# Tiny products of zeros at the start of a scan and expert-layer kernel, and a later line for a load

## The chip, the cores and the metric

The kernel runs on one core of a Trainium2 chip. A core has five engines that run at the same time, each working through its own list of instructions in order: TensorE (PE) multiplies matrices, VectorE (DVE), ScalarE (ACT) and GpSimd (POOL) work element by element, and SyncE (SP) mostly issues transfers (DMAs) between the main memory and the core's own. Engines wait for each other through semaphores. A product on PE is a weight load (shown as PEld) and a matmul that streams columns through the loaded weights; in fp32 each product is made in two such passes.

The metric is the device time of one execution in microseconds. The kernel before takes 350.53 us, the median of three runs (350.33 to 351.12).

## The reference

Inputs are x (4 batches, 8 heads, 768 steps, 32 wide), a (one decay per step), B and C (16 wide), and two weights, w_in (256 x 2048) and w_out (2048 x 256). All is fp32.

```python
for c in range(S // 32):                      # the scan, per batch and head
    cum = np.cumsum(log_a[c])
    L = np.exp(cum[:, None] - cum[None, :]) * causal
    y_intra = ((C_c @ B_c.T) * L) @ x_c
    y_inter = (C_c @ state) * np.exp(cum)
    y[c] = y_intra + y_inter
    state = exp(sum(la)) * state + sum_j(B_j x_j * exp(cum[-1] - cum_j))
h = y_as_rows @ w_in                          # 3072 rows of 256
g = np.where(h > 0, h, np.exp(np.minimum(h, 0)) - 1)
out = g @ w_out
```

So a scan along the sequence makes 3072 rows of 256 numbers, and a two-layer network with an elu in between is applied to every row.

## The kernel before, in words

The 3072 rows are cut into twelve blocks of 256 steps, numbered n = 0 to 11; `place(n)` gives batch and third of the sequence. Within a block the scan works in chunks of 64 steps (Q) for all eight heads. For a block it needs B and C turned so that their 16 columns lie along partitions (`turn`, L422, or `turn_square`, L446), the decays L (`first_decays`, L505, for blocks 0 and 1 and `decay_of`, L518, later), the scores C times B (`scores`, L532), which are weighed by L (`weigh`, L547), the new states (`sums`, L562, and `states`, L578), and then the two halves of y: `across` (L604) with the state from before the chunk and `inside` (L624) with the weighed scores. `scores`, `sums`, `across` and `inside` are bursts of many small products, each on its own part of PE's array: one block's `inside` is 32 products, which are 64 weight loads and 64 matmuls in the trace; for two blocks, and in two steps t, it is 64 and 64 for each t.

The network follows block by block. `l1` (L659) and, from block 2 on in two-block pairs, `l1_words` (L777) make h; the elu is spread over ACT and DVE; `l2` (L820) and `second` (L866) make the output, the latter by a scheme of seven products of quarters.

No scheduler orders the work: inside `tc.manual_schedule()` each engine carries out its instructions in the order in which the source names them. Waits come from the reuse of buffers and from the data.

Three places matter here.

**The start.** L257 to L268 make a tile of zeros (`idle`), whose products PE computes into a bank that nobody reads: `idle_product(4)` and `idle_product(3)`, with 512 and 384 columns. On PE they stand ahead of the first scan: `first_low` (L475, its products are L481), `first_cum` (L486, products L492 and L500), the turned decays of `turned` (L360, product L364) and `turn` (L422, products L428). Beside them DVE computes the running sum of log a (L320), and then takes PE's results: L369 (eb), L436 (the masked C), L550 (`weigh`), and, in the same order, the conversion of the weights (L231, L223, L238). POOL adds the two halves of a converted weight at L248, which `l1` (product L667) waits for. A third `idle_product(3)` stands at L1001.

**The pairs of blocks.** From L1302 on, pair n is put through l1_words and second in sixteen steps k = 0 to 15, and the scan of the next pair m = n + 2 is woven in: at k = 9 `scores`, `sums`, `weigh_two` and the first `states`, at k = 13 `across` and `inside` with eight matmuls of `second` between the bursts.

**The loads.** `stage_scan` (L1282) issues the scan's transfers and ACT's decays for the next pairs. At k = 10 it issues, for both blocks of the pair after the next (m + 2 and m + 3), `load_b` (L135, tile `b`, two buffers) and `spread_cum` (L377, tile `L`, two buffers). They are issued from SP, which carries them out when the buffer's last readers are done: for `b` the products of `sums` (L571), for `L` the products of `weigh` on DVE.

Of the kernel before, what the change touches and what calls it, by code (L numbers as in the profile page):

```python
# [18 lines left out]
Q = 64  # L19
# [13 lines left out]
def kernel(  # L33
# [27 lines left out]
    nc = tc.nc  # L61
# [3 lines left out]
    NP = NB * NG  # L65
# [26 lines left out]
    for k in range(4):  # L92
        (nc.scalar if k % 2 else nc.sync).dma_start(
            out=la0[BH * k:BH * (k + 1)],
# [26 lines left out]
    def load_bc(n, c_queue=nc.sync, us=(0, 1)):  # L121
        b, g = place(n)
        if "bc" not in st.setdefault(n, {}):
            st[n]["bc"] = raw.tile([P, 2, 2, NH, N], F32, tag="bc", name="bc", bufs=2)
        if n > 3:
            for k in range(2):
                load_squares(n, k)
            return
        for u in us:
            sl = slice((2 * g + u) * P, (2 * g + u + 1) * P)  # L130
            for k, src in enumerate((B,) if n == 1 else (B, C)):
                (nc.sync, c_queue)[k].dma_start(
                    out=st[n]["bc"][:, k, u], in_=src[b, :, sl, :].rearrange("h s n -> s h n"))

    def load_b(n):  # L135
        b, g = place(n)
        st.setdefault(n, {})["b"] = raw.tile([P, 2, NH, N], F32, tag="b", name="b_tok", bufs=2)
        for u in range(2):
            sl = slice((2 * g + u) * P, (2 * g + u + 1) * P)
            nc.sync.dma_start(  # L140
                out=st[n]["b"][:, u], in_=B[b, :, sl, :].rearrange("h s n -> s h n"))

    def load_x(n, piece=None):
        b, g = place(n)
        st[n]["x"] = raw.tile([P, 2, NH * D], F32, tag="xr", name="xr", bufs=3)
        for u in range(2):
            sl = slice((2 * g + u) * P, (2 * g + u + 1) * P)
            nc.sync.dma_start(
                out=st[n]["x"][:, u].rearrange("p (h d) -> p h d", d=D),
                in_=x[b, :, sl, :].rearrange("h s d -> s h d"))  # L150
            if piece is not None and u == 0:
                w_load(piece)
# [104 lines left out]
    idle = att.tile([P, P], F32, tag="M", name="idle", bufs=8)  # L257
    nc.vector.memset(idle, 0.0)
    ps_idle = p_o.tile([P, 4, P], F32, tag="o", name="ps_idle")

    def idle_product(k):

        nc.tensor.matmul(
            out=ps_idle[:, 0:k], lhsT=idle, rhs=idle.unsqueeze(1).to_broadcast([P, k, P]),
            start=True, stop=True)

    idle_product(4)
    idle_product(3)  # L268
    ident = const.tile([P, P], F32, name="ident")
    make_identity(nc, ident)  # L270
# [8 lines left out]
    for v in range(2):  # L279
        nc.gpsimd.affine_select(  # L280
            out=low16[Q * v:Q * v + Q], in_=low16[Q * v:Q * v + Q], pattern=[[1, Q]],
# [5 lines left out]
        out=hmask, in_=hmask, pattern=[[-N, NH]], compare_op=ALU.is_ge, fill=0.0,  # L287
        base=0, channel_multiplier=1)
    nc.gpsimd.affine_select(
        out=hmask, in_=hmask, pattern=[[N, NH]], compare_op=ALU.is_ge, fill=0.0,  # L290
# [8 lines left out]
        out=minus, in0=ident, scalar1=-1.0, scalar2=None, op0=ALU.mult)  # L299
# [77 lines left out]
    def spread_cum(n):  # L377

        st.setdefault(n, {})["L"] = L = att.tile([P, NH, 2, Q], F32, tag="L", name="L", bufs=2)
        b, g = place(n)  # L380
        for v in range(2):
            nc.sync.dma_start(
                out=L[Q * v:Q * v + Q].rearrange("p h u i -> p (h u i)"),
                in_=flat[g, v, NH * b:NH * (b + 1)].rearrange("h u i -> (h u i)").unsqueeze(
                    0).to_broadcast([Q, NH * P]))

    def spread_exp(n):

        st.setdefault(n, {})["ec"] = ec = att.tile([P, 2, P], F32, tag="ec", name="ec", bufs=4)
        nc.sync.dma_start(  # L390
            out=ec.rearrange("p u i -> p (u i)"),
            in_=flat_exp[rows_of(n)].unsqueeze(1).to_broadcast([NH, N, BLK]))
# [9 lines left out]
    def scaled(n, eng):  # L402

        s = st[n]
        s["sc"] = sc = s["b"] if n > 3 else raw.tile(
            [P, 2, NH, N], F32, tag="b", name="sc", bufs=2)
        factor = eb0[:, :, NH * n:NH * (n + 1)] if n < 2 else eb[:, :, rows_of(n)]
        eng.tensor_tensor(
            out=sc, in0=s["b"] if n > 3 else s["bc"][:, 0],
            in1=factor.unsqueeze(3).to_broadcast([P, 2, NH, N]), op=ALU.mult)  # L410
# [107 lines left out]
    def decay_of(n, h):  # L518
        L, row = st[n]["L"], rows_of(n).start + NG * h
        for u in range(2):  # L520
            nc.scalar.activation(  # L521
                L[:, h, u], L[:, h, u], ACT.Exp, bias=ncum[:, u, row:row + 1])
        if h % 4 == 3:
            for v in range(2):
                part = L[Q * v:Q * v + Q, h - 3:h + 1]
                nc.gpsimd.affine_select(  # L526
                    out=part, in_=part, pattern=[[0, 4], [0, 2], [1, Q]],
                    compare_op=ALU.is_ge, fill=0.0, base=0, channel_multiplier=-1)
# [753 lines left out]
    def stage_scan(n, k):  # L1282

        m = n + 2
        if k < 2:
            spread_exp(m + k)
        if k == 2:
            load_x(m)
            load_x(m + 1)
        heads = ((5 + 3 * k) // 2, (8 + 3 * k) // 2) if n == 4 else (2 * k - 2, 2 * k)  # L1290
        for h in range(*heads) if 0 < k < 9 else ():
            decay_of(m + h // NH, h % NH)
        if k in (7, 8):
            scaled(m + k - 7, nc.gpsimd)
        if k in (6, 7) and m + 2 < NP:
            load_bc(m + k - 4)
        if k == 10 and m + 2 < NP:
            for to in (m + 2, m + 3):
                load_b(to)
                spread_cum(to)  # L1300

    for n in range(4, NP, 2):  # L1302
        m = n + 2 if n + 2 < NP else None
# [6 lines left out]
        for k in range(16):  # L1310
# [9 lines left out]
            if m:  # L1320
                stage_scan(n, k)
# [64 lines left out]
```

## Time and profile before

| | |
|---|---|
| median of three runs | 350.53 us (350.33 to 351.12) |
| the profiled execution, own time | 350.53 us |
| its span, first to last instruction | 348.6 us |
| PE busy | 341.0 us (98%) |
| DVE, ACT, POOL busy | 257.9, 234.7, 216.5 us |
| instruction queues | q8 30 packets, q14 17 packets |
| PE's products of zeros, first two | 1.10 to 4.45 us |

A line of a timeline gives the start, the length, the engine, the line of the source, the operation, the tiles written and read, the shape, the number of instructions, and in brackets the engine's idle time before it and what ended it. A line of the list of waits gives who waited for whom, the time in all, how often, and the longest. Group lines end with the busy time, the mean duration in ns, and the idle time before. A busy PE is not a PE at its peak: matmuls overlap, and their ends are modelled.

### The profile page before, as it was taken

How to read it: one execution, taken by the hardware profiler on the slowest of the kernel's cores; microseconds unless marked ns; L12 is line 12 of the kernel's file. 1: busy time of each engine (PE TensorE's matmuls, PEld its weight loads, DVE VectorE, ACT ScalarE, POOL GpSimd, SP SyncE). 2: the span in 40 equal slices, each digit the busy share in tenths (PEclk: the TensorE clock that was granted, in tenths of full speed). 3: DMA queues.
4: the chain of work that ended last, by engine and by line, in shares of the span. 5: the costliest groups of instructions: out<-in, count | busy, mean ns of one | idle time of the engine just before them, and what ended most of it. 6: DMA issues, size and time to landing. Idle time of an engine off the chain costs nothing.

```text
span 348.6 us, 9875 instructions
## 1 busy us (share of the span) xinstructions
PE 341.0 (98%) x3878; PEld 298.4 (86%) x3878; DVE 257.9 (74%) x515; ACT 234.7 (67%) x537; POOL 216.5 (62%) x338
## 2 busy tenths in 40 slices
PE   8899999999999999999999999999999999999996
PEld 5579888888778899888999888899988999999996
DVE  3998989889997899876788675878775756665232
ACT  4789989598658988557599457599457466565000
POOL 5554554539998699965296665196754174455760
PEclk9999999999999999999999999999999999999999
DMA  8988989371360510170421070420000100001002
GB/s 146 240 214 173 294 168 261 86 140 42 66 139 0 129 40 17 18 152 2 108 60 32 9 156 7 105 34 2 2 0 5 62 0 3 0 0 51 14 0 62
DMA packets 72727, 26.49 MB, mean 76 GB/s; under 512 B 57768, under 2 KB 67560, under 8 KB 72680
## 3 DMA queue, kind: packets, MB, share of 16 engines
q1 hardware_dynamic: 70360, 25.60, 31.8%
q8 instruction: 30, 0.49, 0.6%
q10 hardware_dynamic: 2320, 0.26, 0.6%
q14 instruction: 17, 0.14, 0.1%
HBM read 22.51 MB, written 3.34 MB: 74 GB/s over the span
## 4 chain that ended last, share of the span: by engine, by line
PE 87%; ACT 3%; DVE 3%; SPq 2%; DMA 2%; issue 1%; POOL 0%; POOLq 0%; ACTq 0%
PE ps_o L902 36%; PE ps_h L787 18%; PE ps_h L667 11%; PE ps_w L787 9%; PE ps_o L827 6%; PE ps_y L634 2%; DMA w<-in_moe_w_in_dram 2%; PE ps_g L541 2%; PE ps_y L616 1%; PE ps_st L571 1%; DVE ps_h L794 1%; ACT e L800 1%; SPq L178 1%; ACT yT L651 1%; ACT e L801 1%
## 5 line engine op out<-in xcount | busy, mean ns | idle before, releaser
L902 PEld LDWEIGHTS ps_o<-w_out,g 128*128 128x128 f32 x640 | 78.5, 191 | 3.5
L902 PE MATMUL ps_o<-w_out,g 128*128 128x128 f32 x640 | 80.1, 275 | 0.0
L800 ACT ACTIVATE e<-ps_h 128x512 f32<-128x512 f32 x72 | 43.0, 597 | 47.2 <-DVE ps_h L794 47.2
L808 DVE SCALAR_TENSOR_TENSOR g<-e,ps_h 128x512 f32<-128x512 f32 x72 | 49.3, 685 | 31.9 <-ACT e L801 30.4
L843 POOL TENSOR_TENSOR g<-g 128x256 f32<-128x256 f32 x36 | 27.3, 758 | 58.5 <-DVE g L808 58.4
L794 DVE SCALAR_TENSOR_TENSOR ps_h<-ps_h,e 128x512 f32<-128x512 f32 x72 | 50.1, 695 | 13.2 <-ACT e L791 10.3
L791 ACT ACTIVATE e<-ps_w 128x512 f32<-128x512 f32 x72 | 42.2, 586 | 20.1 <-PE ps_w L787 20.0
L787 PE MATMUL ps_w<-y_both,w_words 128*128 128x512 f32 x144 | 51.7, 438 | 0.1
L801 ACT ACTIVATE e<-e 128x512 f32<-128x512 f32 x72 | 45.5, 632 | 2.3
L667 PE MATMUL ps_h<-yT,w_in 128*128 128x256 f32 (+1 forms) x208 | 45.1, 367 | 1.6 <-POOL w_in L248 1.6
L787 PE MATMUL ps_h<-y,w_words 128*128 128x512 f32 x144 | 45.7, 399 | 0.0
L787 PE MATMUL ps_h<-y,w 128*128 128x512 f32 x144 | 45.0, 392 | 0.0
L667 PEld LDWEIGHTS ps_h<-yT,w_in 128*128 128x128 f32 x208 | 36.4, 190 | 7.2 <-POOL w_in L248 2.3
L521 ACT ACTIVATE L<-L,ncum 128x64 f32<-128x64 f32 x160 | 42.2, 336 | 0.1
L902 PE MATMUL ps_o<-w_sum,g 128*128 128x128 f32 x304 | 38.6, 276 | 0.0
L902 PEld LDWEIGHTS ps_o<-w_sum,g 128*128 128x128 f32 x304 | 37.0, 192 | 1.4
L526 POOL TENSOR_SCALAR_AFFINE_SELECT L<-L 64x512 f32<-64x512 f32 x40 | 29.3, 733 | 8.0 <-ACT L L521 6.7
L787 PEld LDWEIGHTS ps_h<-y,w 128*128 128x128 f32 x144 | 27.0, 188 | 7.0 <-POOL w L843 0.4
L787 PEld LDWEIGHTS ps_h<-y,w_words 128*128 128x128 f32 x144 | 26.6, 188 | 6.2 <-issue 0.5
L843 POOL TENSOR_TENSOR g<-t,g 128x256 f32<-128x256 f32 x40 | 28.2, 737 | 5.8 <-PE ps_o L902 5.7
L827 PE MATMUL ps_o<-w_out,g 128*128 128x256 f32 x128 | 30.4, 381 | 0.0
L843 POOL TENSOR_TENSOR g<-g,t 128x256 f32<-128x256 f32 x40 | 28.6, 748 | 0.2
(133 smaller groups left out, 536.5 us busy)
## 6 DMA issues: line engine op xcount, KB each, us to landing
L<-flat SPq DMA_DIRECT2D x20, 256.0 KB
w<-in_moe_w_out_dram SPq DMA_DIRECT2D x8, 512.0 KB
w<-in_moe_w_in_dram SPq DMA_DIRECT2D x7, 512.0 KB
xr<-in_x_dram SPq DMA_DIRECT2D x24, 128.0 KB
out_dram<-c_sum SPq DMA_DIRECT2D x9, 256.0 KB
bc<-in_B_dram SPq DMA_DIRECT2D x24, 64.0 KB
bc<-in_C_dram SPq DMA_DIRECT2D x22, 64.0 KB
ec<-flat_exp SPq DMA_DIRECT2D x10, 128.0 KB
```

Source lines behind the costliest of these rows:

```text
L521: nc.scalar.activation(L[:, h, u], L[:, h, u], ACT.Exp, bias=ncum[:, u, row:row + 1])
L526: nc.gpsimd.affine_select(out=part, in_=part, pattern=[[0, 4], [0, 2], [1, Q]], compare_op=ALU.is_ge, fill=0.0, base=0, channel_multiplier=-1)
L667: nc.tensor.matmul(out=ps[:, j, toks], lhsT=w_in[i][:, k, j * P:(j + 1) * P], rhs=yT[n // 2][:, k, n % 2].rearrange("p u i -> p (u i)")[:, ...
L787: nc.tensor.matmul(out=ps, lhsT=lhs[:, k], rhs=rhs[:, k], start=k == 0 and lhs is not w0, stop=k == KC - 1 and lhs is not w1)
L791: nc.scalar.activation(e, both, ACT.Copy, scale=WORD)
L794: nc.vector.scalar_tensor_tensor(out=high, in0=high, scalar=WORD - 1.0, in1=e, op0=ALU.mult, op1=ALU.add)
L800: nc.scalar.activation(e, high, ACT.Relu, scale=-1.0)
L801: nc.scalar.activation(e, e, ACT.Exp, scale=-1.0)
L808: nc.vector.scalar_tensor_tensor(out=g_of[n, m].rearrange("p b i -> p (b i)"), in0=e, scalar=1.0, in1=h, op0=ALU.subtract, op1=ALU.max)
L827: nc.tensor.matmul(out=o_of[n][:, ts], lhsT=g_of[n, j][:, m % 2, ts * P:(ts + 1) * P], rhs=w_out[:, m], start=(m == 0 and ts == 0), stop=( ...
L843: nc.gpsimd.tensor_tensor(out=out, in0=in0, in1=in1, op=ALU.subtract)
L902: nc.tensor.matmul(out=ps[:, ts], lhsT=b[:, ts * P:(ts + 1) * P], rhs=a[:, i], start=(i == chunk[0] and ts == 0), stop=(i == chunk[-1]), s ...
```

## The change

Two edits. The first product of zeros has 384 columns instead of 512, and behind it stand 29 new products of zeros: weights of 32 rows and 64 columns, 16 columns streamed, in turn into the upper and the lower half of the columns of the array. Each is an fp32 product, so it puts four records into PE's list, 116 in all. The other edit moves the loads of `b` and `L` for the pair after the next from step 10 to step 13 in the source.

```diff
+    def small_idle_products(count):
+
+        for k in range(count):
+            cols = slice(Q * (k % 2), Q * (k % 2) + Q)
+            nc.tensor.matmul(
+                out=ps_idle[cols, 0, 0:16], lhsT=idle[0:32, 0:Q], rhs=idle[0:32, 0:16],
+                start=True, stop=True, tile_position=(0, Q * (k % 2)), skip_group_check=True)
+
-    idle_product(4)
+    idle_product(3)
+    small_idle_products(29)
     idle_product(3)
...
-        if k == 10 and m + 2 < NP:
+        if k == 13 and m + 2 < NP:
             for to in (m + 2, m + 3):
                 load_b(to)
                 spread_cum(to)
```

## The prediction

> **What bounds the kernel now.** I read the page first, then the list of waits, then PE's timeline at the waits, then the start of PE and DVE.
>
> ```profile
> PE 341.0 (98%) x3878; PEld 298.4 (86%) x3878; DVE 257.9 (74%) x515; ACT 234.7 (67%) x537; POOL 216.5 (62%) x338
> ...
> q8 instruction: 30, 0.49, 0.6%
> ...
> PE 87%; ACT 3%; DVE 3%; SPq 2%; DMA 2%; issue 1%; POOL 0%; POOLq 0%; ACTq 0%
> ```
>
> PE is the bound: 98% busy, 87% of the chain that ended last. Queue q8 brings instructions: 30 packets of 16,384 bytes (0.49 MB). PE idles in few places, and two lines of the list of waits hold them:
>
> ```profile
> PE ps_y L634 <- issue: 1.6, 4, 0.6
> ...
> PE ps_h L667 <- POOL w_in L248: 1.6, 3, 0.8
> ```
>
> The first is what the change aims at. "issue" means that the engine waited for nothing that the profile shows. PE's timeline at the second of the four (start, length, instruction):
>
> ```profile
> 156.88 0.86 PE L634 MATMUL ps_y<-M,xr 64*32 64x64 f32 x64
> 157.66 0.71 PE L902 MATMUL ps_o<-w_sum,g 128*128 128x128 f32 x4
> 158.31 0.48 PE L634 MATMUL ps_y<-M,xr 64*32 64x64 f32 x33
> 159.14 0.46 PE L634 MATMUL ps_y<-M,xr 64*32 64x64 f32 x31 [0.35 <-issue]
> 159.53 0.73 PE L787 MATMUL ps_w<-y_both,w_words 128*128 128x512 f32 x2
> ```
>
> Two equal bursts of `inside`; the second breaks off after 33 of 64. I counted PE's records (weight loads, products, waits) up to each of the four breaks: 2753, 4033, 5313, 6593, that is 1280 = 5 x 256 apart, and 256 records of 64 bytes are one packet of q8. The packets that start ahead of the breaks do so at 100.56, 156.54, 209.38 and 262.21 us, and the breaks end 2.90, 2.60, 2.34 and 2.72 us later (103.46, 159.14, 211.72, 264.93). So I read: PE's records come in blocks of 256, the next block is fetched when PE enters one, some 3.5 us pass from the crossing until it can be used (about 0.9 to the packet, then these 2.3 to 2.9), and only `across` and `inside` burn 256 records faster.
>
> The start, PE's timeline again:
>
> ```profile
> 1.10 3.35 PE L263 MATMUL ps_idle<-idle 128*128 128x512 f32 x4 [1.10 <-DVE idle L258]
> 4.25 1.06 PE L481 MATMUL ps_x<-low,ident 128*128 128x256 bf16 x4
> 5.24 1.16 PE L492 MATMUL ps_x<-first,ident 32*64 32x128 f32 x32
> 6.33 1.03 PE L500 MATMUL ps_x<-minus,first 32*128 32x128 f32 x16
> 7.19 0.25 PE L364 MATMUL ps_eb<-ident,first 32*128 32x32 f32 x2
> ...
> 15.29 0.60 PE L481 MATMUL ps_x<-low,ident 128*128 128x256 bf16 x4
> 15.82 0.69 PE L492 MATMUL ps_x<-first,ident 32*64 32x128 f32 x32
> 16.44 0.73 PE L500 MATMUL ps_x<-minus,first 32*128 32x128 f32 x16
> ...
> 23.02 1.99 PE L667 MATMUL ps_h<-yT,w_in 128*128 128x256 f32 x8 [0.49 <-POOL w_in L248]
> ```
>
> The same work takes 1.06 us at 4.25 and 0.60 at 15.29: the array runs at half rate first. The products of L263 start 849 and 638 ns apart for 512 and 384 columns, 1.66 ns a column; later 256 columns take 214 ns, 0.84 a column. The trace's clock record has full rate from 7.01 us on.
>
> DVE's timeline shows who waits for this start:
>
> ```profile
> 7.50 0.23 DVE L369 TENSOR_SCALAR eb<-ps_eb 128x64 f32<-128x64 f32 x1 [1.99 <-PE ps_eb L364]
> ...
> 15.77 0.70 DVE L231 TENSOR_SCALAR ps_mag<-ps_mag 128x512 f32<-128x512 f32 x1 [0.16 <-ACT ps_mag L196]
> ```
>
> From 7.50 to the mag of L238 at 20.80 DVE works in order nearly without a hole; that mag releases POOL's L248 at 21.64 and this PE at 23.02, and then PE has no gap over 0.06 us until 103. So what delays L364 delays everything, less DVE's one hole of 0.16.
>
> **The change part by part.**
>
> Load moved from step 13 instead of 10: nothing. In what is built, every engine has the same instructions in the same order, SP included (no other transfer lies between the two steps), and every wait is for the same event; only counts of PE's semaphore are 29 higher. The loads are released by PE's L571 and the readers of L, as before. Bounds 0 and 0.
>
> The shift. 29 fp32 products are 58 weight loads and 58 products, 116 records; the smaller first product keeps its records. In the old numbering the block edges move from 193+256k to 77+256k. Old times of the new edges round the four places: 92.29, 102.03, 108.28; 150.38, 157.30, 165.29; 204.18, 210.03, 217.07; 258.25, 262.97, 270.88. The closest pair anywhere is 4.7 us, above 3.5, so all four breaks should go. Worth: the unbroken burst lasts 157.66 - 156.88 = 0.79 to the next instruction; the broken ones 1.22 (159.53 - 158.31), 1.17 (212.30 - 211.13) and 1.34 (265.32 - 263.99). Gain 0.43 + 0.38 + 0.55 = **1.36 us**, with PE the chain behind each. The first break (0.56) I cost at nothing: ACT and DVE bound that stretch.
>
> ```profile
> 103.13 0.63 ACT e L801
> 103.76 0.26 ACT yT L651
> ```
>
> ACT goes from L801 straight into six copies that end at 105.96; those of the second burst begin at 104.8, when PE had been done since 104.3, and PE waits for y_both at 115.3 anyway. Were that cover gone, 0.65 more is gained.
>
> The Trainium skill (Runtime: NRT & Kernel Launch, Instruction fetch mechanics) also has blocks of 16 KiB, 256 instructions, but gives PE room for 2048 and calls a crossing mostly hidden. By it the breaks are no fetches, the gain is 0, and the sum below is 353.6; the spacing of 1280 records speaks against it.
>
> The tiny products. Old: streaming from 1.27, L481 at 4.25. New, at half rate: two passes of 384 columns, 1.28, to 2.54; the change of shape 0.14 (L481 to L492: 349 ns apart, of which 212 stream), 2.68. Then 58 pairs of a 64-column load and a 16-column product, on two column halves in turn. No row shows a product shorter than its load. The loads by shape:
>
> ```profile
> L902 PEld LDWEIGHTS ps_o<-w_out,g 128*128 128x128 f32 x640 | 78.5, 191 | 3.5
> ...
> L616 PEld LDWEIGHTS ps_y<-bct,Sx 32*64 32x64 f32 x352 | 5.0, 131 | 2.5 <-POOL Sx L593 1.6 <-POOL w_sum L843 0.3
> ```
>
> 64 columns more cost 60 ns at full rate, and in L616's first round the second product of a tile starts 54 ns after its load does. So a load of 64 columns streams for 54 ns, 107 at half rate, and the next product on that half must wait for it; the two halves overlap, as the tiles of L634 do (8 products in 56 ns). 29 rounds of 0.11 = 3.2 us. Bounds: 0.4 (58 at L634's 6.7 ns) and 6.2 (58 x 107, halves not overlapping). I take 3.2, since two tiles, not eight, are in turn and the load is the longer part. The products end at 5.87; with 0.16 out of the shape, 0.21 for a full load and 1.28 for the second product(3), L481 starts at 7.55 if the clock is still at half rate, 3.3 later than 4.25.
>
> The clock decides the rest. Before the switch PE had streamed from 1.27 to 7.01, 5.7 us. The new stretch from 2.7 to 6.3 streams 16 columns per load, a quarter to a half of the time. If that counts as work, the switch stays at 7.0: the second product ends at 7.28, L481, L492 and L500 take 0.53 + 0.62 + 0.66 = 1.81 as at 15.29, L364 is at 9.1, 1.9 late. If it doesn't, they take about 2.9 as before and L364 is at 10.4, 3.25 late; with a full 5.7 us from 6.27 the switch would come at 12.0 and cost up to 0.9 more. I take 3.25: work at a third of the rate is nearer to none. Less DVE's 0.16: **+3.1 us**.
>
> The Trainium skill (TensorE: Matmul & The Clock Gate, Part 1) says that the gate looks at free-running windows of 3413 ns and opens after a busy one. The trace agrees: full rate lasted 341.33 us, 100 windows. By it the window 0.18 to 3.59, with PE streaming for 68%, did not suffice, and a missed one at 7.01 means 10.42.
>
> Sum: the profiled execution took 350.53 (span 348.6, 1.9 round it), which is also the median. 350.53 - 1.36 + 3.1 = **352.3 us**. A measurement tells about 0.2%, 0.7 us, from no change.
>
> **Rivals.**
>
> Clock on time: 350.53 - 1.36 + 1.9 - 0.16 = 350.9. For it: weight loads run all the time. Against: the columns streamed.
>
> Faster: the tiny products pass at burst pace, because loads on a quarter of the rows do not hold up the next product. At 0.4 to 0.85 us (6.7 ns as L634, 14.6 as L616) L481 comes 0.5 to 0.9 late, the clock stays at 7.0, and L364 is about 0.6 late: 350.53 - 1.36 + 0.4 = 349.6. It decides when the 58 pairs take under about 1.0 us. For it: all bursts in the trace run so. Against: those use four or eight tiles and products at least as long as their loads.
>
> Halves take turns: 6.2 us of tiny products. L364 is 5.2 late: 354.2. For it: both halves read the same 32 rows. Against: L634 overlaps four column tiles on the same rows.
>
> The shift doesn't do what it says (the breaks belong to the burst, or others open at the new edges): 352.3 + 1.36 = 353.6. The spacing of 1280 speaks against it.
>
> **How the numbers follow.** Forecast 0.40 (alone 351.6 to 353.2), clock on time 0.20, burst pace 0.22, halves in turn 0.11, no gain 0.07. Forecast, halves and no gain are slower: 0.58. Burst pace is faster but for its upper end: 0.20. The clock rival and that upper end are the same: 0.22. The range leaves out most of the halves in turn and the lower part of burst pace: 349.4 to 353.8.
>
> **What would show it.** Right: no "issue" wait at L634; L481 first at about 7.5 and L364 near 10.4 against 7.19; L481's first four at half rate; DVE's L369 3 us late; the rest shifted as a block, about 1.7 later at the end. Wrong: L481 before 5.5 (burst pace), L492 at 0.69 us length (clock on time), a break in L541, L571 or L634 at another place (edges), or PE's waits at 23 gone, so that the start has slack that I don't see.

## The result and the profile after

The changed kernel takes 352.73 us, the median of six executions (352.14 to 353.53); the kernel before, measured beside it, 350.87 (350.33 to 351.12). The ratio is 1.0057, with a 95% interval of 1.0042 to 1.0072: slower by about 1.9 us. The profiled execution took 352.14, with a span of 350.4.

From the page of the changed kernel (busy time by engine, the instruction queue, the chain that ended last):

```profile
PE 344.0 (98%) x3936; PEld 300.5 (86%) x3936; DVE 257.5 (73%) x515; ACT 234.6 (67%) x537; POOL 216.6 (62%) x338
...
q8 instruction: 31, 0.51, 0.6%
...
PE 86%; ACT 6%; DVE 4%; POOL 3%; issue 1%; POOLq 0%
```

PE has the 58 matmuls more and one packet of instructions more. ACT has twice its old share of the chain that ends last, 6% for 3%. That is the first hint that something other than PE sets a part of the end.

The list of waits, of the changed kernel:

```profile
PEld ps_w L796 <- DVE y_both L781: 2.9, 7, 0.5
...
PE ps_h L676 <- POOL w_in L248: 1.6, 3, 0.8
```

and the line of the same list of the kernel before that answers to the first:

```profile
PEld ps_w L787 <- DVE y_both L772: 1.2, 3, 0.4
```

(The source lines are nine higher in the changed kernel.) No wait for "issue" stands at the products of `inside` (L643): all four breaks are gone. But PE's weight loads now wait for DVE's `y_both` seven times and 2.9 us, not three times and 1.2.

PE's timeline of the changed kernel, its start (start, length, engine, line and so on, as in the timelines before):

```profile
1.10 1.65 PE L263 MATMUL ps_idle<-idle 128*128 128x384 f32 x2 [1.10 <-DVE idle L258]
2.68 3.38 PE L271 MATMUL ps_idle<-idle 32*64 32x16 f32 x58
5.99 1.65 PE L263 MATMUL ps_idle<-idle 128*128 128x384 f32 x2
7.43 1.06 PE L490 MATMUL ps_x<-low,ident 128*128 128x256 bf16 x4
8.42 0.94 PE L501 MATMUL ps_x<-first,ident 32*64 32x128 f32 x32
9.29 0.73 PE L509 MATMUL ps_x<-minus,first 32*128 32x128 f32 x16
9.84 0.25 PE L373 MATMUL ps_eb<-ident,first 32*128 32x32 f32 x2
...
25.67 1.99 PE L676 MATMUL ps_h<-yT,w_in 128*128 128x256 f32 x8 [0.49 <-POOL w_in L248]
```

The tiny products run from 2.68 to 5.99. The first line of the scan (L490) starts at 7.43, where it started at 4.25. Full rate comes at 9.00 by the trace's clock record, in the middle of L501, so only part of the slow stretch is added: the product for `eb` is at 9.84, 2.65 late, and the last `l1` that waits for POOL's weights, at 25.67, is still 2.65 late. In the next burst of `across` this falls to 2.3, and from there the two executions run side by side, PE 2.2 to 2.3 behind.

Then come the four places of the breaks. The difference between the two traces at the same product of PE (changed minus before) goes like this:

| place | just before | behind the old break | behind the next turn to `y_both` |
|---|---|---|---|
| first, 103 | 2.31 | 1.57 | 2.34 |
| second, 159 | 1.99 | 1.48 | 2.16 |
| third, 212 | 2.16 | 1.75 | 2.16 |
| fourth, 265 | 2.16 | 1.44 | 1.84 |

Every break is gained, 0.4 to 0.7 us, and at the first three all of it is given back some ten us later, where PE waits for `y_both`, which DVE makes from the copies of y for the products of the next pair (at the first place PE waits for `y` too, made the same way); only the fourth leaves 0.3. At the end the changed kernel is 1.8 behind by its span, 1.6 by the two profiled times.

ACT's timeline of the changed kernel at the second place shows why:

```profile
160.30 0.63 ACT L810 ACTIVATE e<-e 128x512 f32<-128x512 f32 x1
160.84 2.29 ACT L660 COPY yT<-ps_y 128x256 f32<-128x256 f32 x6
163.16 0.60 ACT L800 ACTIVATE e<-ps_w 128x512 f32<-128x512 f32 x1
```

DVE's timeline of the same stretch:

```profile
163.79 0.70 DVE L803 SCALAR_TENSOR_TENSOR ps_h<-ps_h,e 128x512 f32<-128x512 f32 x1 [2.13 <-ACT e L800]
...
169.17 1.28 DVE L781 SCALAR_TENSOR_TENSOR y_both<-y,yT 128x512 fp32r<-128x512 f32 x2
```

and PE's:

```profile
169.90 1.10 PE L796 MATMUL ps_w<-y_both,w_words 128*128 128x512 f32 x2
```

ACT copies both bursts of y out of PSUM in one unbroken run of six, right behind its work for the elu. It starts when L810 is done, not when PE is done, and DVE idles 2.13 us behind it. In the kernel before, the same six copies begin at 158.56 and take the same 2.29, with a break in PE's burst beside them. ACT's timeline of the kernel before:

```profile
158.03 0.63 ACT L801 ACTIVATE e<-e 128x512 f32<-128x512 f32 x1
158.56 2.29 ACT L651 COPY yT<-ps_y 128x256 f32<-128x256 f32 x6
```

So ACT and DVE arrive at `y_both` at the same distance with the break or without it. PE's two products from `y_both` (L796 at 169.90) took 0.62 in the kernel before, at 168.22, back to back; now they take 1.10, because the weight loads of both wait (0.39 and 0.42).

### The profile page after: what moved, and what is told of

Same layout as the page of the kernel before. It is cut to its first block, busy times and chain, and to the rows that moved or that the text cites. A ratio compares the mean times of both kernels' runs of the same rounds, so it can differ in the third digit from the quotient of the medians.

```text
span 350.4 us, 9991 instructions
## 1 busy us (share of the span) xinstructions
PE 344.0 (98%) x3936; PEld 300.5 (86%) x3936; DVE 257.5 (73%) x515; ACT 234.6 (67%) x537; POOL 216.6 (62%) x338
## 4 chain that ended last, share of the span: by engine, by line
PE 86%; ACT 6%; DVE 4%; POOL 3%; issue 1%; POOLq 0%
PE ps_o L911 34%; PE ps_h L796 16%; PE ps_h L676 11%; PE ps_w L796 9%; PE ps_o L836 5%; PE ps_y L643 2%; PE ps_g L550 2%; ACT yT L660 1%; PE ps_y L625 1%; DVE ps_h L803 1%; PE ps_idle L263 1%; DVE y_both L781 1%; PE ps_st L580 1%; PE ps_idle L271 1%; ACT e L809 1%
## 5 line engine op out<-in xcount | busy, mean ns | idle before, releaser
L796 PE MATMUL ps_w<-y_both,w_words 128*128 128x512 f32 x144 | 52.4, 440 | 0.4
L810 ACT ACTIVATE e<-e 128x512 f32<-128x512 f32 x72 | 45.5, 632 | 2.3
L796 PE MATMUL ps_h<-y,w_words 128*128 128x512 f32 x144 | 45.7, 398 | 0.0
L796 PE MATMUL ps_h<-y,w 128*128 128x512 f32 x144 | 45.3, 393 | 0.2
L796 PEld LDWEIGHTS ps_h<-y,w 128*128 128x128 f32 x144 | 27.0, 188 | 7.8 <-issue 0.9
L796 PEld LDWEIGHTS ps_h<-y,w_words 128*128 128x128 f32 x144 | 26.6, 188 | 6.3 <-issue 0.4
```

The source lines that it names most:

```text
L796: nc.tensor.matmul(out=ps, lhsT=lhs[:, k], rhs=rhs[:, k], start=k == 0 and lhs is not w0, stop=k == KC - 1 and lhs is not w1)
L810: nc.scalar.activation(e, e, ACT.Exp, scale=-1.0)
```

## The experiments

Each run was measured against the kernel before on the same chip; ratios are to it. Differences between two runs are taken from their ratios, at 350.6 us for 1. The first four runs had a median of 350.4 for the kernel before, the last four 350.61.

**The load at step 13 alone.** The tiny products are left out.

```diff
-        if k == 10 and m + 2 < NP:
+        if k == 13 and m + 2 < NP:
```

> Only the later line for the loads (step 13, not 10); the start as before. Theory: nothing that is built moves, so the time is within 0.2% of the kernel before (350.2 to 351.5), and the four breaks in inside stand where they were, 0.56, 0.35, 0.16 and 0.50 us. Rival (the loads land later and collide with something else): a change of 0.5 us or more either way, and b or L landing at other times.

Measured: 350.61 us, ratio 1.0006 (0.9992 to 1.0021), no difference. The breaks stand at the same products as before, 0.75, 0.65, 0.22 and 0.50 long here.

This run also shows something about the start. The array came to full rate at 4.94 us, not at 7.01, with the same products ahead of it. `eb` was ready 0.9 earlier, and still `l1` at 23.25 was 0.2 later than before. ACT's timeline of this run:

```profile
15.51 0.64 ACT L196 ACTIVATE ps_mag<-w 128x512 f32<-128x512 f32 x1 [1.57 <-DMA w<-in_moe_w_in_dram]
```

ACT waits there for the transfer of a piece of the weights, which in the kernel before ended a wait of 0.65 at 15.10. In this execution the earlier clock won nothing at the start, because that transfer was later than the products.

**The same shift with a cheaper start.** Of the 29 tiny products, each takes a quarter of the columns in turn instead of a half, with a load of 32 columns; 116 records as before.

```diff
-            cols = slice(Q * (k % 2), Q * (k % 2) + Q)
+            cols = slice(32 * (k % 4), 32 * (k % 4) + 32)
...
-                out=ps_idle[cols, 0, 0:16], lhsT=idle[0:32, 0:Q], rhs=idle[0:32, 0:16],
-                start=True, stop=True, tile_position=(0, Q * (k % 2)), skip_group_check=True)
+                out=ps_idle[cols, 0, 0:16], lhsT=idle[0:32, 0:32], rhs=idle[0:32, 0:16],
+                start=True, stop=True, tile_position=(0, 32 * (k % 4)), skip_group_check=True)
```

> As the changed kernel, but the 29 tiny products go in turn to four quarters of the columns with weights of 32 columns, so that a load is half as long and four stand in turn. The shift of 116 records is kept. Theory (a tiny product waits for the load of its own weights): 58 pairs take 58 / 4 x 0.055 = 0.8 us instead of 3.3, the first scan product (L490 in the changed kernel) starts at 5.1 instead of 7.43, eb's product at about 8.0 instead of 9.84 since the clock is up earlier, no break in inside, and the end is about 1.5 earlier than the changed kernel: 351.0 to 351.4. Rival (each pair has a fixed cost, whatever its tile): the stage stays at 3 us and the time at 352.7.

Measured: 350.83 us, ratio 1.0017 (1.0003 to 1.0032). That is 1.4 us less than the changed kernel, and a little under the expected range. PE's timeline:

```profile
2.68 1.03 PE L271 MATMUL ps_idle<-idle 32*32 32x16 f32 x58
3.64 1.65 PE L263 MATMUL ps_idle<-idle 128*128 128x384 f32 x2
5.08 1.06 PE L490 MATMUL ps_x<-low,ident 128*128 128x256 bf16 x4
```

The stage falls from 3.3 to 0.96 us. The length of the loads, the number of tiles that take turns, or both set what a tiny product costs here: the run changes the two at once and does not tell them apart. No break is left, and still the kernel is not faster than before. The product for `eb` is 1.0 late in this profile, so 1.36 from the breaks should have left it ahead.

**256 records.** The same quarters, but 64 products, so that the shift is one whole block and every edge falls where it was.

```diff
-    small_idle_products(29)
+    small_idle_products(64)
```

> As the run with quarters, but 64 tiny products, 256 records, one whole block. Theory (blocks of 256 records): the four breaks are back in inside after the same products as in the kernel before, 0.2 to 0.6 us each; the start takes 0.9 to 1.0 more than with 29. What the four breaks cost by themselves is read from the offsets in the trace: about 0.3 to 0.5 if ACT and DVE cover most of them, 1.4 if PE bears three in full. Time 352.0 to 352.6 or 353.0 to 353.5. Rival (the breaks depend on how many records stand ahead, not on the block): no breaks, and the time is that of 29 plus 0.9.

Measured: 351.69 us, ratio 1.0042 (1.0027 to 1.0057), under both expected ranges. PE's list of waits has the breaks again:

```profile
PE ps_y L643 <- issue: 1.5, 3, 0.8
```

and PE's timeline shows one of them at the place of before, between the 33rd and the 34th product of the second burst:

```profile
159.58 0.48 PE L643 MATMUL ps_y<-M,xr 64*32 64x64 f32 x33
160.27 0.46 PE L643 MATMUL ps_y<-M,xr 64*32 64x64 f32 x31 [0.21 <-issue]
```

All four stand at exactly the products of before, 0.51, 0.21, 0.79 and 0.10 long (the list leaves the shortest out). So the breaks belong to the places of the records modulo 256: the reason given for the shift is right. The Trainium skill (Runtime: NRT & Kernel Launch, Instruction fetch mechanics) has the blocks of 256 too, and calls the cost of crossing from one to the next mostly hidden. In these runs breaks of 0.10 to 0.81 us stand at such crossings, in the bursts where PE takes its records fastest.

Against the run with 29 quarters, product by product, PE is 1.08 ahead of it at 86 us, ahead of the first break, and 0.81 ahead at 276, behind the last (ahead, although its scan started 0.9 later, since the other run waited until 17.6 for a transfer of weights; more on that below). At the four places it loses 0.75, 0.40, 1.00 and 0.30, and another 0.4 in `sums` at 146, between the first and the second; all but 0.27 in all comes back, most of it where the other run waits for `y` and `y_both`. So four breaks cost this kernel about 0.3 us net by these two traces. The medians are 0.86 apart, which the later start alone would make, so they show no more than that.

**No tiny products, a full stream instead.** Two products of 512 columns replace the 29, so the shift is of 8 records and nothing moves off the edges.

```diff
-    small_idle_products(29)
+    idle_product(4)
+    idle_product(4)
```

> The tiny products are replaced by two full products of 512 columns each, 3.4 us at half rate, about as long as the tiny ones (3.3); 8 records more than before, so the breaks stay near their old places. Theory (the clock counts streamed work): full rate from 8.1 us at the latest instead of 9.0, the first scan product at 7.2, eb's product at 8.2 to 9.2 instead of 9.84, and the end between 351.6 and 352.6. Rival (the clock comes on after a time that the tiny products did not change): full rate at 9 or later, eb's product at 9.6, the end at 353.0.

Measured: 351.17 us, ratio 1.0022 (1.0012 to 1.0033). PE's timeline:

```profile
1.10 5.11 PE L263 MATMUL ps_idle<-idle 128*128 128x384 f32 x8 [1.10 <-DVE idle L258]
6.05 0.60 PE L491 MATMUL ps_x<-low,ident 128*128 128x256 bf16 x4
...
7.75 0.25 PE L374 MATMUL ps_eb<-ident,first 32*128 32x32 f32 x2
```

With a streaming array the clock opened at 4.84, after the first window that was streamed throughout, and the scan ran at full rate from its first product. (At 4.94 and 4.88 it opened as early in two executions with the products of the kernel before, so the place of the windows may have had a part in this too.) `eb`'s product and the time came earlier than the range expected for them. Three breaks are there, 0.59 at the first place, 0.26 and 0.51 at the last two; at the second none is over 0.06. These three stand at the same records as before, 2753, 5313 and 6593, and so four products earlier in the burst, because 8 records more stand ahead: the break goes with the record and not with the product. The kernel is still faster than the changed one.

**The cheapest shift.** The quarters, with 256 columns instead of 384 in the two products around them, so that L490 starts where L481 did.

```diff
-    idle_product(3)
+    idle_product(2)
     small_idle_products(29)
-    idle_product(3)
+    idle_product(2)
```

> The shift by 116 records with the cheapest start that the runs so far allow: 29 tiny products on four column quarters with loads of 32 columns, 2.7 us at most at half rate, and two products of 512 and 384 columns less around them than in the run with quarters. Theory (the breaks of bursts 1 to 3 are given back where PE waits for y_both, only the last nets about 0.3; the start costs what the first L481 line is late): L481's first at 4.3 to 4.4 us, as in the kernel before (4.25), the four breaks gone, PE's wait for y_both near 2.9 in all as in the changed kernel, time 0.2 to 0.5 below the kernel before, 350.4 to 350.7. Rival (the breaks' full price of 1.36 is gained and the start hid it): 349.5.

Measured: 350.32 us, ratio 0.9994 (0.9977 to 1.0011). (The edit takes 128 columns out of each of the two products, not whole products of 512 and 384 columns, as the expectation has it.) L490 is at 4.23, the breaks are gone, and the list of waits reads

```profile
PEld ps_w L796 <- DVE y_both L781: 2.9, 7, 0.5
```

as in the changed kernel. The rival's 349.5 lies outside the interval. The start is not quite free: `eb`'s product came at 7.32, against 7.19, 6.29 and 6.27 in the three profiles with the start of the kernel before. With that included, four breaks less bring 0.3 us in the median, and nothing that the measurement can tell from none.

**The copies of the second burst on DVE, in the changed kernel.** If ACT's run of six copies is what covers the breaks, half of it can go to DVE, which idles behind it.

```diff
-                    if t and n == 1:
+                    if t and (n == 1 or n > 3):
                         nc.vector.tensor_copy(to, src)
                     else:
                         nc.scalar.copy(out=to, in_=src)
```

> The changed kernel, but the three yT copies of the second burst of the later pairs go to DVE, which idles 2.1 us there, and not to ACT. Theory (ACT's six copies of 2.29 us are what holds L791, then DVE, then y_both, so that PE waits for y_both the longer the earlier its burst ends): ACT's L791 comes about 1.1 earlier after each burst, DVE's L794 some 0.7 earlier, PE's wait for y_both falls from 2.9 to under 1, and the time falls from 352.7 to 350.9 to 351.6. Rival (PE's own order or DVE's later work sets y_both, and the copies are only beside it): the wait stays over 2 and the time at 352.4 to 353.0.

Measured: 350.83 us, ratio 1.0002 (0.9984 to 1.002), just under the expected range: 1.9 us less than the changed kernel, and the intervals do not touch. ACT's timeline:

```profile
162.05 1.12 ACT L660 COPY yT<-ps_y 128x256 f32<-128x256 f32 x3
163.20 0.60 ACT L800 ACTIVATE e<-ps_w 128x512 f32<-128x512 f32 x1
```

and DVE's:

```profile
162.35 1.31 DVE L658 COPY yT<-ps_y 128x256 f32<-128x256 f32 x3 [0.84 <-PE ps_y L643]
163.69 0.69 DVE L817 SCALAR_TENSOR_TENSOR g<-e,ps_h 128x512 f32<-128x512 f32 x1
```

and PE's wait, from the list:

```profile
PEld ps_w L796 <- DVE y_both L781: 0.8, 2, 0.4
```

The second burst's copies now begin when PE releases them. Only the first turn, at 118, still waits. The profiled execution itself started 1.4 later than that of the changed kernel, for the clock came to full rate at 12.27 there, and ended 0.5 earlier by the span.

**The same copies in the kernel before.** The breaks stay.

> The kernel before, but with the three yT copies of the second burst of the later pairs on DVE; the breaks stay. Theory (as in the run on the changed kernel): the wait for y_both, 1.2 in three, goes, and the time falls by 0.5 to 1.1, to 349.8 to 350.4, less than the copies bring in the changed kernel, because here the breaks delay the second burst's copies. Rival: the wait stays and the time is within 0.2 of 350.9.

Measured: 350.16 us, ratio 0.9989 (0.9967 to 1.0011). From the list of waits:

```profile
PE ps_y L634 <- issue: 2.3, 4, 0.8
```

The median is where the theory put it, but its distance from no change is less than the measurement tells. PE's wait for `y_both` did not go altogether: it fell from 1.2 us in three to 0.8 in two, both in the first turn. The breaks, 0.76, 0.23, 0.81 and 0.52 here, now delay the copies on DVE, which wait 6.1 us for PE's `ps_y` in four, against 3.0 in the run that follows.

**Both.** The cheapest shift with the copies on DVE; the two products of 256 columns around the tiny ones stay here too.

> Both: the cheap shift of the quarters without the two extra products, and the second burst's copies on DVE. Theory (the cover gone, the breaks' price is now gained): 1.0 to 1.7 below the kernel with the copies alone, so 348.5 to 349.5, no break at L634, and no wait for y_both over 1 us in all. Rival (breaks are still covered by something else): within 0.4 of the kernel with the copies alone.

Measured: 348.40 us (347.62 to 349.00), ratio 0.9933 (0.991 to 0.9956). It beats both kernels, and the interval lies clear of both single steps and of 1. The time is just under the expected range.

| median, us | breaks in place | breaks gone |
|---|---|---|
| six copies on ACT | 350.61 | 350.32 |
| three of them on DVE | 350.16 | 348.40 |

The shift is worth 0.3 with ACT's copies in the way and 1.8 without. Both numbers hold the start's remaining cost too: in the two profiles of the lower row PE is 0.6 behind at 25 us, then gains 0.96, 0.36, 1.08 and 0.71 at the four places, and less than 0.2 comes back behind each. PE's list of waits of this last run is short:

```profile
PE ps_h L676 <- POOL w_in L248: 1.6, 3, 0.8
PE ps_idle L263 <- DVE idle L258: 1.1, 1, 1.1
```

## Why the prediction came out

The time came within 0.5 us of the forecast, 352.73 for 352.3, and the sign and the side of the rivals were right. But two of its terms, of opposite sign, were too large and cancelled, so that it came this close is luck.

**The load at step 13** was costed at nothing, and is nothing: the run with that edit alone measured 1.0006 with an interval on both sides of 1.

**That the shift removes the breaks** was right. They belong to blocks of 256 records, 116 records clear all four, 256 bring them back at the same products, 8 move them by four products, and no other edge opened a break over 0.06 us. One reading behind it is loose. By the times at which the records start, the packet comes 0.7 to 0.9 after the crossing at the last three places, and the break ends 3.2 to 3.5 after the crossing. At the first place the packet starts 0.6 ahead of it (100.56, and 101.17 for record 2497), and the break ends 2.3 after it. In the run with the full stream the packet came 0.5 after the crossing at the second place, and PE passed the next edge 2.9 after it without a break. So 3.5 us is not a fixed time, and when the packet starts may have a part in how long PE waits.

**What the breaks are worth, 1.36 us, was wrong.** This is the step that failed: it costed the second to fourth break "with PE the chain behind each", and only the first at nothing, because there "ACT and DVE bound that stretch". Much the same chain bounds all four. At the second place ACT runs from L801 straight into six copies at 158.56, as it does at the first at 103.76, and behind the third PE waited for `y_both` in the kernel before already (0.42 at 221.4). Only at the fourth did ACT's copies wait for PE, for 0.15. Behind the second place PE had no such wait before and has 0.8 us of it (0.39 and 0.42) now: the break and the slack had just cancelled. The profiles showed 0.74, 0.51, 0.41 and 0.72 gained at the four and 0.77, 0.68, 0.41 and 0.40 given back: net 0.1 at the four places, and 0.5 with the 0.35 that the kernel before lost between the first and the second, most of it in `sums` (1.21 us at 144, now 0.86). The cheapest shift measured 0.3 in the median. With the copies off ACT the price of the breaks appears, 1.8 with the cost of the start inside it. That the forecast was near is therefore no proof of this part.

**The tiny products, 3.2 us, were right.** One round of two halves takes 107 ns in the trace, which is the estimate for a load of 64 columns at half rate; the stage took 3.3, and L490 was at 7.43 for 7.55. That the load is what the round waits for was not tested alone. The rival of burst pace (under 1.0 us) and that of halves in turn (6.2) both fell. The quarters show what the former would have needed: four tiles in turn and loads half as wide gave 0.96.

**The clock, "L364 is at 10.4, 3.25 late", was right in kind and mis-sized.** The stretch of tiny products did not open the clock, as forecast, but full rate came at 9.00, not at 10.42, since the windows lay otherwise in that execution; `eb` was 2.65 late. In the run with the copies on DVE, with the same instructions at the start, full rate came at 12.27 and `eb`'s product at 10.52. So the size of this term differs from execution to execution, and the forecast's 3.25 lies near the later of the two seen (3.33).

**That the delay is passed on whole, less 0.16** held to 23 us, and the 0.16 was not even saved there: the hole closed (L231 is 2.41 late), but DVE's next instruction, L223, took 0.85 us and not 0.59, and 2.65 stood again. From 69 us on it was 2.2 to 2.3. The hole of 0.16 was the visible end of ACT's wait of 0.65 for a transfer. That wait also fits what the run with the later loads alone showed: a start that was 0.9 earlier won nothing there.

So the sum as it came, by the two traces: 2.65 from the start, 0.3 to 0.4 of it absorbed by 69 us, less 0.3 to 0.5 from the breaks and what lies between them, 1.8 in the span, for 3.1 less 1.36.

## What to carry to other kernels

A gap of an engine is worth its length only if what ends next, behind it, was waiting for that engine: look at the other engines' timelines at every place where the gap occurs, not at one, and see whether their work moves when the gap does. A gap that is followed by no wait may have used up slack that comes back as a wait once it is closed. Padding that shifts instruction records is paid at the start, where the clock is low and everything waits; load few columns, over as many tiles as there are, and take the columns out of products that are there anyway.

## What the runs showed of the hardware

**Breaks at block edges vary in length.** The four places showed 0.56, 0.35, 0.16 and 0.50 in the kernel before, 0.75, 0.65, 0.22 and 0.50 with the load at step 13 alone, 0.51, 0.21, 0.79 and 0.10 with 256 records more. The places are fixed by the records; the length differs by up to 0.65 us from one execution to the next (the third was 0.81 in the kernel before with the copies on DVE), and with the full stream the second was absent.

**The clock's start depends on a phase that differs from execution to execution.** Full rate began at 7.01, 4.94 and 4.88 in three kernels with the same products at the start, and at 9.00 and 12.27 in two others with the same products. The Trainium skill (TensorE: Matmul & The Clock Gate, Part 1) says that the windows of 3413 ns run freely and that the change varies with where in one the first product falls; the traces agree, since a full-rate stretch lasts 341.33 us, 100 windows, in the changed kernel and before, and 99 or 101 in others.

**Windows with much of their time in tiny products did not open the clock.** Taking the windows back from the moment of full rate, the one from 5.59 to 9.00 in the changed kernel, with 0.40 us of tiny products and then 3.0 of streaming (88%), opened the clock; the one from 5.45 to 8.86 in the run with the copies on DVE, with 0.54 of tiny products (84% streamed), did not. Windows that were streamed throughout opened it at once (4.84, 4.94). A window with 2.91 us of tiny products in the changed kernel (2.18 to 5.59) did not open it either. That the tiny products count for nothing at all, and that the limit lies between 84% and 88%, is an inference from these windows; a stretch of tiny products longer than a window was not tried.

**A late transfer can cover it all.** ACT waited for a piece of the weights at 15.51 (1.57 us) in the run with the later loads alone, whose clock came early, and not at all in the changed kernel, where it got there at 17.00. In the profiled executions of the run with quarters and of the cheapest shift the same piece came as late as 17.6 and 17.5, and these were the slowest executions of their kernels, 352.04 and 352.05 against medians of 350.83 and 350.32. Why that transfer lands at 15.1 in one execution and at 17.6 in another was not settled.
